# One fused attention and MLP kernel: the first group's load cut in two, and the third output block postponed in the last steps

## The chip, the cores and the metric

The kernel runs on one core of one Trainium2 chip. The metric is the device time of one execution in microseconds (us), here the median of several. Three runs of the kernel before gave 478.76, 478.81 and 479.46 us, so the median is 478.81 us.

## The reference

A linear attention with decay runs over 768 positions for 4 batches and 8 heads of width 48. Its output, 3072 rows of 384 numbers, goes through an MLP: a product to 2048 hidden numbers, an exact GELU, and a product back to 384.

```
for t in range(S):
    cur = np.einsum('bhd,bhe->bhde', u[None] * kt, vt)
    y[:, :, t] = np.einsum('bhd,bhde->bhe', rt, state + cur)
    state = w[None, :, :, None] * state + np.einsum('bhd,bhe->bhde', kt, vt)
h = x @ w_in
g = 0.5 * h * (1.0 + erf(h * inv_sqrt2))
return (g @ w_out).astype(np.float32)
```

All inputs and the output are 32-bit floats.

## The kernel before

The 768 positions are cut into 6 chunks of 128 positions; a chunk with its 4 batches is 512 rows, the free size of a matmul. Attention runs in groups, one for two heads in one chunk, so a chunk has four groups. The MLP runs in 96 steps, 16 for each chunk, one for each block of 128 hidden numbers.

**A step of the MLP.** `moe1` makes 9 matmuls of 128x512 (line 695): three blocks of the input, each as a product of high and low parts (`wh` with the high part, `wl` with the high part, `wh` with the low part). They are summed in the one PSUM bank `Hp`. ScalarE applies the GELU twice, to `gh` (rounded, line 725) and to `gf` (full, line 726), and VectorE forms the remainder `gl` (line 727). `moe2` makes 9 more matmuls (line 737) from `gh` and `gl` into the output banks `O0`, `O1`, `O2`, which hold the three blocks of 128 output columns. `moe2` of a step stands behind `moe1` of the next, so that TensorE has work while the GELU runs. In the last chunk the third block lies half in `O2` (256 rows) and half in the bank `Y` (256 rows).

**The end.** In the last steps of the program the third block is left out of `moe2` and done behind the others. In the kernel before this holds for the last four steps (hidden blocks 12 to 15): the line `range(len(parts) if m < NSTEP - 4 else 2)`, and the list of pairs in the branch `m == NSTEP - 1`, where a pair `(q, i)` is block part `i` (0 and 1 are `O0` and `O1`, 2 is `O2`, 3 is `Y`) of the step `q` before the last. Values that are read so late need buffers that no later step writes: `hidden` gives the last three steps parts of `xx0`. When a bank has its last product, ScalarE (line 775) or VectorE (line 772) copies it out and SP issues its transfer to memory (line 778).

**The front.** Before the first MLP step the four groups of the first chunk are computed. For each group SP loads receptances and keys (`T`, 128 partitions by 4 KB, line 263). VectorE multiplies them to `RK` (line 464), TensorE sums `RK` with `u` in `Hp` (line 469), ScalarE copies the sums to `cs` (line 474) and scales a diagonal with them (`Am`, line 414). VectorE also scales `T` by powers of the decay to `Ts` (line 458), TensorE makes scores from that (line 483), and VectorE puts them into `Am` (line 488). The tables `E` are filled by SBUF transfers from `W` (line 365). The MLP weights come as `raw` (line 379) and are split by ScalarE and VectorE into `wh` and `wl`.

**What sets the order.** All work is recorded with `add` and `dma` into a `Plan`, with an estimated duration, a due time and names for what it reads and writes. `Plan.play` then puts it out by engine, the most urgent of the ready operations first. Its DMA estimates are the constants `DMA_*`; a transfer holds one of eight lanes until it has landed, and the ninth waits for the first one's lane. The queue of SP is in order, and so are all engines.

Of the kernel before, what the change touches and what calls it, by code (L numbers as in the profile page):

```python
# [10 lines left out]
F32R = mybir.dt.float32r  # L11
# [27 lines left out]
LATER = 10 ** 7  # L39
FIRST, STEP, STEP_LAST = 27000, 8400, 3900  # L40
WEIGHT_AHEAD, GROUP_AHEAD, GROUP_DUE = 26000, 28000, 18000
HEATS, HEAT_NS, HEAT_ROOM, MM = 10, 300, 100, 233
WIDE = 96
POOL_DUE, POOL_CLASH = 8000, 550
# [4 lines left out]
AT_LOADS, AT_E = 14000, 15000  # L49

SCALE = ("dd", "d", "d", "d")
PRODUCT = ("d", "d", "d", "d")
BONUS = ("aa", "aa", "aa", "ad")


class Plan:
# [6 lines left out]
    LAG = {"pe": 220, "act": 140, "dve": 115, "pool": 90, "sp": 0, "do": 0}  # L63
    DMA_GAP, DMA_LEAD, DMA_FIXED, DMA_LANES = 480, 1050, 950, 8
    DMA_EARLY, DMA_RATES = 5000, (400.0, 345.0)
    DMA_QUEUED, DMA_SPREAD = 1200, 1050

    def __init__(self, after):
        self.after = after
# [39 lines left out]
    def play(self, due):  # L109
# [11 lines left out]
        for _ in ops:  # L121
            best, clash = None, float("inf")
            for e in self.LAG:
                wait, can = waiting[e], able[e]
                if not wait and not can:
                    continue
                start = max(free[e], lanes[0]) if e == "sp" else free[e]
                while wait and wait[0][0] <= start:
                    n = heapq.heappop(wait)[1]
                    heapq.heappush(can, (due[n], n))  # L130
                if can:
                    n = can[0][1]
                else:
                    start = wait[0][0]
                    n = min((due[n], n) for at, n in wait if at == start)[1]
                if e == "dve":
                    clash = start if ops[n][5] else start + ops[n][1]
                if ops[n][5]:
                    start = max(start, locked["pool" if e == "dve" else "dve"])
                if e == "pool" and best and start + ops[n][1] > clash + POOL_CLASH and due[n] > start + POOL_DUE:  # L140
                    continue
                if best is None or start < best[0]:
                    best = (start, e, n)
            start, e, n = best
            while e == "pe" and heating:
                at = {b: max([free[e]] + [clear.get(x, 0.0) for x in b]) for b in self.heats
                      if not any(unread.get(x, 0) for x in b)}
                b = min(at, key=at.get, default=None)
                if b is None or at[b] + self.heat_room >= start:
                    break  # L150
                self.heats[b]()
                free[e] = at[b] + self.heat_ns
            if able[e]:
                heapq.heappop(able[e])
            else:
                waiting[e].remove((ready[n], n))
                heapq.heapify(waiting[e])
            _, ns, _, fn, _, port = ops[n]
            if e == "sp":
                free[e] = start + self.DMA_GAP  # L160
                queued = bus - start - self.DMA_LEAD
                bus = max(bus, start + self.DMA_LEAD) + ns / self.DMA_RATES[start >= self.DMA_EARLY]
                end = bus + self.DMA_FIXED + self.DMA_SPREAD * (queued > self.DMA_QUEUED)
                lanes = lanes[1:] + [end]
            else:
                free[e] = end = start + ns
            ins = fn()
            if port:
                locked[e] = end
                if e == "dve":  # L170
                    held = ins
                elif held is not None:
                    self.after(ins, held, "port")
            if n in (self.heat_from, self.heat_to):
                heating = n == self.heat_from
            if heating:
                for b in [x for bank in self.heats for x in bank]:
                    if b in self.writes[n]:
                        unread[b] = unread.get(b, 0) + sum(b in self.reads[m] for m in self.users[n])
                    if b in self.reads[n]:  # L180
                        unread[b] = unread.get(b, 0) - 1
                        clear[b] = end + self.LAG[e]
            for m in self.users[n]:
                ready[m] = max(ready[m], end + self.lag(n, m))
                left[m] -= 1
                if not left[m]:
                    heapq.heappush(waiting[ops[m][0]], (ready[m], m))


def rwkv_gelu_mlp(tc, rkT, rkv, wuT, uN, wmlp, r, k, vT, w, u, out):  # L190
    nc = tc.nc
    with ExitStack() as ctx:
# [37 lines left out]
        Am = [sb([C, 2, NB, C], F32, f"Am{i}") for i in range(2)] + [sb([C, 2, NB, C], F32, f"Am{i}", pro) for i in (2, 3)]  # L230
        cs = [sb([C, NB * 2], F32, f"cs{i}") for i in range(4)]
        xx = [sb([128, 2, 3, TOK], F32R, f"xx{i}") for i in range(2)]
        x3 = sb([LP, 2, TOK], F32R, "x3")
        gh = [sb([128, TOK], F32R, f"gh{i}") for i in range(2)]
        gl = [sb([128, TOK], F32R, f"gl{i}") for i in range(2)]
        gf = sb([128, TOK], F32, "gf")
# [21 lines left out]
        slot = lambda gi: gi if gi < NP else NP + gi % 2  # L258


        def load_group(gi, at, r=()):
            s = slot(gi)
            dma(C * 4096, at, lambda: nc.sync.dma_start(T[s], rkT[gi]), r=r, w=[f"T{s}"])
            if gi < NP:
                dma(C * 3072, AT_LOADS + 800 * gi, lambda: nc.sync.dma_start(N[s], rkv[gi, :, 1:]), r=r, w=[f"Nk{s}", f"Nv{s}"])
            else:
                dma(C * 4608, at + 1, lambda: nc.sync.dma_start(N[s], rkv[gi]), r=r, w=[f"Nr{s}", f"Nk{s}", f"Nv{s}"])
# [32 lines left out]
        add("act", 520, LATER, spread_ones, r=["ident", "zeros"], w=["spread"])  # L300


        def heat(dst):
            nc.tensor.matmul(dst, lhsT=zeros[:, 0:128], rhs=zeros, start=True, stop=True)

# [6 lines left out]
                out=x.bitcast(F32).rearrange("p (a n) -> p a n", a=2),  # L312
                in_=zeros[:, 0:DM].bitcast(F32).unsqueeze(1).to_broadcast([128, 2, DM])), r=["zeros"], w=["wa"])

        plan.heats, plan.heat_ns, plan.heat_room = {("H",): lambda: heat(Hp), ("O0",): lambda: heat(O[0])}, HEAT_NS, HEAT_ROOM
        plan.heat_from = add("pe", 430 * HEATS, 10, warm_up, r=["zeros"], w=["H", "A0", "A1", "O0", "O1", "O2", "Y", "U"])


        def powers():
# [124 lines left out]
        def first_group(gi, at, XX, XB, y, YB):  # L444
# [8 lines left out]
            for i, e in enumerate(halves):  # L453
# [4 lines left out]
                    lambda mul=mul, bs=bs, nb=nb: mul(  # L458
                        out=t[:, :, bs], in0=T[gi][:LP, :, bs],
                        in1=W[:, p, 0:C].unsqueeze(1).unsqueeze(1).to_broadcast([LP, 2, nb, C]), op=ALU.mult),  # L460
                    r=["P", f"W{p}", f"T{gi}"], w=[f"{TR}{b}" for b in range(bs.start, bs.stop)], port=True)
            me = PRODUCT[gi]
            mul = nc.vector.tensor_tensor if me == "d" else nc.gpsimd.tensor_tensor
            add("dve" if me == "d" else "pool", dve(512) if me == "d" else pool(512), LATER, lambda: mul(
                out=RK[gi], in0=T[gi][:LP, 0, :, ::-1], in1=T[gi][:LP, 1], op=ALU.mult), r=[f"T{gi}"], w=[f"RK{gi}"], port=True)

            def sum_pairs():
                for b in range(NB):
                    nc.tensor.matmul(
                        Hp[:, WIDE * b:WIDE * b + WIDE].rearrange("s (n j) -> s n j", j=2), lhsT=RK[gi][:, b, :],  # L470
                        rhs=u_pair[:, p, :].unsqueeze(1).to_broadcast([LP, WIDE // 2, 2]), start=True, stop=True)

            add("pe", 1070, LATER, sum_pairs, r=[f"RK{gi}", "w_sb"], w=["H"])
            add("act", 110, LATER, lambda: nc.scalar.copy(
                out=sums.rearrange("s (b j) -> s b j", j=2),
                in_=Hp[:, 0:NB * WIDE].rearrange("s (b x) -> s b x", x=WIDE)[:, :, 0:2]), r=["H"], w=[CS])
            for j in range(2):
                bonus(am, AM, diag, ["diag"], C, sums, CS, j, BONUS[gi][j])
            def scores(bs):
# [13 lines left out]

            def gaps():
                for a in range(2):
                    nc.tensor.matmul(y, lhsT=spread[:, p, :], rhs=x3[:, a, :], start=(a == 0), stop=False,
                                     skip_group_check=True)

            def new():
# [197 lines left out]

        def hidden(m):

            if m < NSTEP - 3:  # L700
                return gh[m % 2], gl[m % 2], f"gh{m % 2}", f"gl{m % 2}"
            i, k_ = NCH % 2, NSTEP - 1 - m
            return xx[i][:, 0, k_], xx[i][:, 1, k_], f"xx{i}{k_}h", f"xx{i}{k_}l"

        def moe1(m, at):
# [8 lines left out]
            if m == 0:  # L714
                gaps0 = lambda k_: gaps[2 * k_:2 * k_ + 2]
                for k_ in range(3):
                    first = add("pe", 3 * MM, at + k_, lambda k_=k_: [
                        product1(x, j, n, (k_,), k_ == 0 and n == 0, k_ == 2 and n == 2) for n in range(3)],
                        r=["wh0", "wl0"] + xr("h", (k_,)) + xr("l", (k_,)) + gaps0(k_), w=["H"])
                    plan.heat_to = plan.heat_to or first  # L720
            else:
                for n in range(3):
# [17 lines left out]
        def moe2(m, at, dest):  # L740
# [14 lines left out]
                        go(m, n, which, at + n)  # L755
            elif m < NSTEP - 2:
                for n in range(3):
                    go(m, n, range(len(parts) if m < NSTEP - 4 else 2), at + n + 2000 * (m == NSTEP - 3 and n == 2))
            elif m == NSTEP - 1:
                for q, i in ((1, 0), (1, 1), (3, 2), (3, 3), (0, 0), (0, 1), (2, 2), (1, 2), (0, 2), (2, 3), (1, 3), (0, 3)):  # L760
                    at += 2000
                    for n in range(3):
                        go(m - q, n, (i,), at + n)
# [110 lines left out]
        def swap():  # L874
# [5 lines left out]
            late.tile([128, 8], F32, name="pad")  # L880

        add("do", 0, SWAP_DUE, swap, w=["late", "ident", "ones", "diag", "past", "P", "WKs", "WN", "zeros", "warm", "spread"] +
            [f"{x}{i}" for x in ("W", "T", "RK", "Nk", "Nv") for i in range(NP)] +
            [f"Ts{i}{b}" for i in range(NP) for b in range(NB)] + [f"Am{i}{j}" for i in (2, 3) for j in range(2)])

        def step_at(m):
            return FIRST + STEP * min(m, 5 * NJ) + STEP_LAST * max(m - 5 * NJ, 0)
# [116 lines left out]
```

## Time and profile before

| | before |
|---|---|
| median of 3 runs | 478.81 us |
| profiled execution, its own time | 479.26 us |
| its span | 477.4 us |
| TensorE busy | 469.3 us (98% of the span) |
| VectorE busy | 229.1 us (48%) |
| ScalarE busy | 182.1 us (38%) |
| GpSimd busy | 67.5 us (14%) |
| mean DMA rate | 98 GB/s |

Busy time says little by itself here: an engine that is full over the whole span (TensorE) sets the length of the middle, and the two ends, where it is not full, have to be read by themselves. The granted TensorE clock was 0.999 over the execution. The chain that ended last is by engine 92% TensorE, 4% DMA and 3% ScalarE.

### The profile page before, as it was taken

Reading aid. Unit: us, or ns where it says so; the run is one execution under the profiler, and the core shown is the slowest. Engines: PE = TensorE matmul, PEld = TensorE weight load, DVE = VectorE, ACT = ScalarE, POOL = GpSimd, SP = SyncE. Lnnn points to the kernel's source line nnn. Section 1 sums busy time; section 2 is a strip of 40 time slices with the busy share of each in tenths; the row PEclk is TensorE's granted clock in tenths of the full one; section 3 lists DMA queues with packets and bytes.
Section 4 is the critical chain, followed back from the end, with each engine's and each line's share of the span. In section 5 each row is a group of like instructions: output and inputs, shape, how many; then the busy total and the mean of one; then the engine's idle time right before and its main releaser. Section 6 shows DMA issues by size and latency. Waiting matters only on the chain.

```text
span 477.4 us, 10280 instructions
## 1 busy us (share of the span) xinstructions
PE 469.3 (98%) x4525; PEld 378.5 (79%) x4525; DVE 229.1 (48%) x345; ACT 182.1 (38%) x333; POOL 67.5 (14%) x91
## 2 busy tenths in 40 slices
PE   8999999999999999999999999999999999999995
PEld 6777788888888787888888888888888887888885
DVE  7989989744354366153543543544335311211111
ACT  9998897233222223222223222223322222322221
POOL 1331021221020222010202202202102000000000
PEclk9999999999999999999999999999999999999999
DMA  8979682414023034031231330311402000100002
GB/s 307 364 288 331 215 266 89 122 51 152 27 80 106 2 116 150 1 106 42 65 106 67 95 104 3 106 65 46 158 19 88 14 0 12 66 1 1 1 0 71
DMA packets 15426, 46.60 MB, mean 98 GB/s; under 512 B 3664, under 2 KB 4048, under 8 KB 15376
## 3 DMA queue, kind: packets, MB, share of 16 engines
q1 hardware_dynamic: 15376, 45.88, 28.6%
q8 instruction: 37, 0.61, 0.5%
q14 instruction: 13, 0.11, 0.1%
HBM read 38.73 MB, written 4.72 MB: 91 GB/s over the span
## 4 chain that ended last, share of the span: by engine, by line
PE 92%; DMA 4%; ACT 3%; issue 0%; DVE 0%; ACTq 0%
PE Hp L695 42%; PE O L737 41%; PE Y L605 2%; DMA E<-W 2%; PE A L613 2%; PE Y L633 2%; PE A L622 1%; DMA raw<-in_wmlp_dram 1%; PE Y L737 1%; ACT W L343 0%; ACT Sa L529 0%; ACT wa L311 0%; ACT L290 0%; ACT wa L394 0%; ACT gh L725 0%; ACT gf L726 0%
## 5 line engine op out<-in xcount | busy, mean ns | idle before, releaser
L695 PE MATMUL Hp<-xx,wh 128*128 128x512 f32 x570 | 167.1, 400 | 0.0
L727 DVE TENSOR_TENSOR gl<-gf,gh 128x512 fp32r<-128x512 f32 x93 | 66.1, 710 | 172.9 <-ACT gf L726 172.7
L725 ACT ACTIVATE gh<-Hp 128x512 fp32r<-128x512 f32 x92 | 54.9, 597 | 217.6 <-PE Hp L695 217.6
L695 PEld LDWEIGHTS Hp<-xx,wh 128*128 128x128 f32 x570 | 104.4, 188 | 25.4 <-ACT gf L726 1.0
L695 PE MATMUL Hp<-xx,wl 128*128 128x512 f32 x285 | 82.0, 395 | 0.0
L737 PE MATMUL O<-gh,wh 128*128 128x512 f32 (+1 forms) x279 | 79.1, 391 | 0.6 <-ACT gf L726 0.6
L737 PE MATMUL O<-gh,wl 128*128 128x512 f32 (+1 forms) x279 | 79.2, 391 | 0.0
L737 PE MATMUL O<-gl,wh 128*128 128x512 f32 (+1 forms) x279 | 78.9, 390 | 0.0
L695 PEld LDWEIGHTS Hp<-xx,wl 128*128 128x128 f32 x285 | 53.6, 188 | 12.7
L737 PEld LDWEIGHTS O<-gh,wh 128*128 128x128 f32 x279 | 52.3, 188 | 13.8 <-ACT gf L726 1.0
L737 PEld LDWEIGHTS O<-gh,wl 128*128 128x128 f32 x279 | 51.6, 188 | 11.7
L737 PEld LDWEIGHTS O<-gl,wh 128*128 128x128 f32 x279 | 51.4, 188 | 11.6 <-issue 0.5
L726 ACT ACTIVATE gf<-Hp 128x512 f32<-128x512 f32 x95 | 56.4, 594 | 0.0
L560 POOL TENSOR_TENSOR Nb<-Nb 128x384 f32<-128x384 f32 x20 | 20.3, 1016 | 123.2 <-DMA Nb<-in_rkv_dram 73.8
L557 DVE TENSOR_TENSOR Tb<-Tb,E 112x1024 f32<-112x1024 f32 x20 | 25.3, 1266 | 2.1 <-DMA Tb<-in_rkT_dram 2.1
L662 DVE SCALAR_TENSOR_TENSOR Sb<-Sa,E,A 48x192 f32<-48x192 f32 x40 | 16.5, 413 | 18.1 <-PE A L622 17.5
L432 ACT CAST xx<-Y 112x512 fp32r<-112x512 f32 x15 | 8.8, 586 | 39.0 <-PE Y L633 39.0
L563 POOL TENSOR_TENSOR Nb<-Nb,WN 128x384 f32<-128x384 f32 x20 | 20.3, 1015 | 21.2 <-DVE wl L406 7.8
L566 POOL TENSOR_TENSOR Nb<-Nb,u_sb 128x384 f32<-128x384 f32 x20 | 20.3, 1013 | 18.3 <-DVE gl L727 13.1
L569 DVE TENSOR_REDUCE cs<-Nb 128x8 f32<-128x384 f32 x20 | 11.1, 553 | 18.1 <-POOL Nb L566 15.8
L643 POOL MEMSET done<- 1x1 f32 x19 | 1.7, 88 | 126.1 <-PE Y L605 126.1
L669 DVE COPY_PREDICATED Am<-past,A 128x512 f32<-128x512 uint32 x20 | 15.0, 748 | 7.0 <-PE A L622 6.8
(114 smaller groups left out, 383.4 us busy)
## 6 DMA issues: line engine op xcount, KB each, us to landing
raw<-in_wmlp_dram SPq DMA_DIRECT2D x16, 767.8 KB, 5.9
Nb<-in_rkv_dram SPq DMA_DIRECT2D x20, 576.0 KB, 5.5
Tb<-in_rkT_dram SPq DMA_DIRECT2D x20, 512.0 KB, 4.3
out_dram<-raw SPq DMA_DIRECT2D x5, 768.0 KB, 3.6
T<-in_rkT_dram SPq DMA_DIRECT2D x4, 512.0 KB, 5.0
xx<-x SPq DMA_DIRECT2D x30, 64.0 KB, 4.0
N<-in_rkv_dram SPq DMA_DIRECT2D x4, 384.0 KB, 7.0
out_dram<-raw SPq DMA_DIRECT2D x2, 256.0 KB, 4.3
```

The source lines that it names most:

```text
L557: add("dve", 1140, LATER, lambda: nc.vector.tensor_tensor(out=flat, in0=flat, in1=E[:, p, 0].rearrange("l h i -> l (h i)").unsqueeze(1).to ...
L560: add("pool", pool(DM), LATER, lambda: nc.gpsimd.tensor_tensor(out=n[:, 0], in0=n[:, 0], in1=n[:, 1], op=ALU.mult), r=[NK], w=[NR])
L563: add("pool", pool(DM), LATER, lambda: nc.gpsimd.tensor_tensor(out=kn, in0=kn, in1=WN2[:, p].rearrange("s j d -> s (j d)").unsqueeze(1).to ...
L566: add("pool", pool(DM), LATER, lambda: nc.gpsimd.tensor_tensor(out=n[:, 0], in0=n[:, 0], in1=u_sb[:, p, :].unsqueeze(1).to_broadcast([C, N ...
L569: add("dve", 465, LATER, lambda: nc.vector.tensor_reduce(out=sums, in_=n[:, 0].rearrange("s b (j d) -> s (b j) d", d=D), axis=AX.X, op=ALU ...
L662: add("dve", 430, at, lambda l=l, x=x: nc.vector.scalar_tensor_tensor(out=out[quarter(1 - x)], in0=src[l], scalar=E[l, p, 1, h, 32:33], in ...
L669: add("dve", 625, LATER, lambda: nc.vector.copy_predicated(out=am, mask=past2.bitcast(U32).unsqueeze(1).unsqueeze(1).to_broadcast([C, 2, N ...
L695: nc.tensor.matmul(dst, lhsT=wt[j][:, 0, k_ * 128:(k_ + 1) * 128], rhs=x[:, a, k_, :], start=start and k_ == ks[0], stop=stop and k_ == ks ...
L725: add("act", 480, LATER, lambda: nc.scalar.activation(out=high, in_=dst, func=AF.Gelu, scale=256.0), r=[H_], w=[GH])
L726: add("act", 480, LATER, lambda: nc.scalar.activation(out=gf, in_=dst, func=AF.Gelu, scale=256.0), r=[H_], w=["gf"])
L727: add("dve", dve(512), LATER, lambda: nc.vector.tensor_tensor(out=low, in0=gf, in1=high.bitcast(F32), op=ALU.subtract), r=["gf", GH], w=[G ...
L737: nc.tensor.matmul(dst[:, a:b], lhsT=wt[j][:, 1, d * 128:(d + 1) * 128], rhs=gt[:, a:b], start=(j == 0 and n == 0), stop=(j == NJ - 1 and ...
```

## The change

There are two parts.

*In the front*, the load of `T` for group 0 becomes two transfers of 256 KB, batches 0 and 1 and then batches 2 and 3. In each partition a half is two runs of 1 KB, where the whole was one run of 4 KB. The product `RK` and the sums of group 0 are recorded by halves as well. The names that the planner uses for `T`, `RK` and `H` are now by batch, and the planner's own DMA estimate gets one more constant.

*At the end*, the third block is left out of `moe2` in the last six steps and not four (`LEFT = 6`), and done behind the others. Hidden block 10 is now kept in `x3`, which grows from 112 to 128 partitions for it; blocks 11 and 12 stay in `gh1` and `gh0`.

```diff
+LEFT = 6
-    DMA_QUEUED, DMA_SPREAD = 1200, 1050
+    DMA_QUEUED, DMA_SPREAD, DMA_UNEVEN = 1200, 1050, 550
...
-                end = bus + self.DMA_FIXED + self.DMA_SPREAD * (queued > self.DMA_QUEUED)
+                end = bus + self.DMA_FIXED + (self.DMA_SPREAD if queued > self.DMA_QUEUED else self.DMA_UNEVEN * (ns > 200000))
...
-        x3 = sb([LP, 2, TOK], F32R, "x3")
+        x3 = sb([128, 2, TOK], F32R, "x3")
...
+        halves_of = lambda gi: ((0, 1), (2, 3)) if gi == 0 else (range(NB),)
...
-            dma(C * 4096, at, lambda: nc.sync.dma_start(T[s], rkT[gi]), r=r, w=[f"T{s}"])
+            for bs in halves_of(gi):
+                dma(C * 1024 * len(bs), at, lambda bs=slice(bs[0], bs[-1] + 1): nc.sync.dma_start(
+                    T[s][:, :, bs], rkT[gi, :, :, bs]), r=r, w=[f"T{s}{b}" for b in bs] if gi < NP else [f"T{s}"])
...
-            add("dve" if me == "d" else "pool", dve(512) if me == "d" else pool(512), LATER, lambda: mul(
-                out=RK[gi], in0=T[gi][:LP, 0, :, ::-1], in1=T[gi][:LP, 1], op=ALU.mult), r=[f"T{gi}"], w=[f"RK{gi}"], port=True)
...
+            for bs in halves_of(gi):
+                sl, Tn, Rn = slice(bs[0], bs[-1] + 1), [f"T{gi}{b}" for b in bs], [f"RK{gi}{b}" for b in bs]
+                add("dve", dve(128 * len(bs)), LATER, lambda sl=sl: nc.vector.tensor_tensor(
+                    out=RK[gi][:, sl], in0=T[gi][:LP, 0, sl, ::-1], in1=T[gi][:LP, 1, sl], op=ALU.mult),
+                    r=Tn, w=Rn, port=True)
+                add("pe", 268 * len(bs), LATER, lambda bs=bs: sum_pairs(bs), r=Rn + ["w_sb"], w=[f"H{b}" for b in bs])
...
-            if m < NSTEP - 3:
+            i, k_ = NCH % 2, NSTEP - 1 - m
+            if k_ == 5:
+                return x3[:, 0], x3[:, 1], "x3h", "x3l"
+            if k_ >= 3:
                 return gh[m % 2], gl[m % 2], f"gh{m % 2}", f"gl{m % 2}"
...
-                    go(m, n, range(len(parts) if m < NSTEP - 4 else 2), at + n + 2000 * (m == NSTEP - 3 and n == 2))
+                    go(m, n, range(len(parts) if m < NSTEP - LEFT else 2), at + n + 2000 * (m == NSTEP - 3 and n == 2))
...
-                for q, i in ((1, 0), (1, 1), (3, 2), (3, 3), (0, 0), (0, 1), (2, 2), (1, 2), (0, 2), (2, 3), (1, 3), (0, 3)):
+                for q, i in ((1, 0), (1, 1), (5, 2), (4, 2), (0, 0), (0, 1), *((q, 2) for q in range(LEFT - 3, -1, -1)),
+                             *((q, 3) for q in range(LEFT - 1, -1, -1))):
```

In the order of instructions the change touches few places. On SP, at the start, the first five transfers were

```order
1 L269 DMA wu_sb_73<-in_wuT_dram 112x12
2 L263 DMA T0_93<-in_rkT_dram 128x1024
3 L263 DMA T1_94<-in_rkT_dram 128x1024
4 L263 DMA T2_95<-in_rkT_dram 128x1024
5 L265 DMA N0_107<-in_rkv_dram 128x768
```

and they are now

```order
1 L273 DMA wu_sb_73<-in_wuT_dram 112x12
2 L266 DMA T0_93<-in_rkT_dram 128x2x256 x2
3 L266 DMA T1_94<-in_rkT_dram 128x1024
4 L266 DMA T2_95<-in_rkT_dram 128x1024
5 L269 DMA N0_107<-in_rkv_dram 128x768
```

One transfer more stands ahead of all the others, whose order is unchanged. On VectorE, at the same place, `RK0` stood between the reciprocals of the decay powers as one instruction

```order
11 L332 RECIPROCAL W_89<-W_89 112x64
12 L464 TENSOR_TENSOR RK0_103<-T0_93 112x512
13 L332 RECIPROCAL W_89<-W_89 112x64 x3
14 L458 TENSOR_TENSOR Ts0_99<-T0_93,W_89 112x2x256 x2
15 L464 TENSOR_TENSOR RK1_104<-T1_94 112x512
```

and now stands there as two. ScalarE and GpSimd keep their order in the front, and TensorE too.

On TensorE, at the end, behind the last products of `O1` for hidden block 14 (`wh14`, `wl14`) there stood

```order
L737 MATMUL O2_72<-gh0_124,wh12_450 128x256
L737 MATMUL O2_72<-gh0_124,wl12_451 128x256
L737 MATMUL O2_72<-gl0_126,wh12_450 128x256
L737 MATMUL Y_68<-gh0_124,wh12_450 128x256
L737 MATMUL Y_68<-gh0_124,wl12_451 128x256
L737 MATMUL Y_68<-gl0_126,wh12_450 128x256
L737 MATMUL O0_70<-xx0_121,wh15_456 128x512
L737 MATMUL O0_70<-xx0_121,wl15_457 128x512
L737 MATMUL O0_70<-xx0_121,wh15_456 128x512
```

and now there stand

```order
L746 MATMUL O2_72<-x3_123,wh10_448 128x256
L746 MATMUL O2_72<-x3_123,wl10_449 128x256
L746 MATMUL O2_72<-x3_123,wh10_448 128x256
L746 MATMUL O2_72<-gh1_125,wh11_450 128x256
L746 MATMUL O2_72<-gh1_125,wl11_451 128x256
L746 MATMUL O2_72<-gl1_127,wh11_450 128x256
L746 MATMUL O0_70<-xx0_121,wh15_458 128x512
L746 MATMUL O0_70<-xx0_121,wl15_459 128x512
L746 MATMUL O0_70<-xx0_121,wh15_458 128x512
```

Six products of 256 rows stand there as before, for other hidden blocks. Behind the last product of `O1` there follow 9 products of `O2` and 9 of `Y` before, and 12 of `O2` and 18 of `Y` now. The 12 products more are those that left the `moe2` of hidden blocks 10 and 11; the number of matmuls is the same.

## Rows read from the trace of the kernel before

**Rows 1.** The page's head.

```profile
span 477.4 us, 10280 instructions
```

**Rows 2.** By stretch: length, busy PE, PEld, DVE, ACT, POOL, PEclk, DMA share, GB/s.

```profile
32.00:36.00 4.00, 4.00 (x78) 3.13 (x77) 3.67 (x8) 3.84 (x6) 2.47 (x3) 1.00 0.26 56
```

**Rows 3.** Chain that ended last, the front: start us, us, what.

```profile
7.75 11.30 DMA E<-W
...
19.06 5.94 DMA raw<-in_wmlp_dram
...
25.02 1.10 ACT wa L394
...
31.02 0.50 ACT gf L726
...
31.56 0.96 PE O L737 x3
```

**Rows 4.** Timeline of the front: start us, us, engine, what [idle before <-releaser].

```profile
5.13 0.69 DVE L464 TENSOR_TENSOR RK<-T 112x512 f32<-112x512 f32 x1 [0.50 <-DMA T<-in_rkT_dram]
...
5.90 1.12 PE L469 MATMUL Hp<-wu_sb,RK 112*128 112x96 f32 x8
...
6.98 0.50 ACT L286 COPY past<-past 64x64 f32<-64x64 f32 x2
...
7.50 0.17 ACT L474 COPY cs<-Hp 128x8 f32<-128x8 f32 x1
...
10.24 1.30 DVE L488 COPY_PREDICATED Am<-past,A 128x1024 f32<-128x1024 uint32 x1 [0.25 <-ACT Am L414]
```

**Rows 5.** DMA queue: packets, MB, share of 16 engines; at 5-5.5, 16-18, 474-474.5 us.

```profile
q1 hardware_dynamic: 54, 0.21, 103.6%
...
q1 hardware_dynamic: 1685, 0.60, 122.4%
...
q1 hardware_dynamic: 138, 0.13, 76.5%
```

**Rows 6.** Chain that ended last, the end.

```profile
457.68 2.09 PE Hp L695 x9
...
461.17 2.14 PE Hp L695 x9
...
471.41 1.07 PE Y L737 x9
```

**Rows 7.** Issues of the first and last output transfer, and their us to landing.

```profile
470.31 0.34 SPq L778 DMA_DIRECT2D out_dram<-raw  x1
out_dram<-raw SPq DMA_DIRECT2D x1, 256.0 KB, 4.4
...
472.99 0.51 SPq L778 DMA_DIRECT2D out_dram<-Nb  x1
out_dram<-Nb SPq DMA_DIRECT2D x1, 128.0 KB, 2.9
```

**Rows 8.** Page, DMA issues (KB each, median us to landing); stretches as in Rows 2.

```profile
out_dram<-raw SPq DMA_DIRECT2D x5, 768.0 KB, 3.6
xx<-x SPq DMA_DIRECT2D x30, 64.0 KB, 4.0
...
108.00:108.50 0.50, 0.50 (x4) 0.41 (x3) 0.00 (x0) 0.50 (x2) 0.00 (x0) 1.00 0.99 381
...
474.00:474.50 0.50, 0.00 (x0) 0.00 (x0) 0.00 (x0) 0.00 (x0) 0.00 (x0) 1.00 0.77 264
```

**Rows 9.** DMA queues at 474.5-475 us, then at 475-475.5 us.

```profile
q1 hardware_dynamic: 13, 0.01, 8.4%
q14 instruction: 1, 0.01, 7.1%
...
q8 instruction: 1, 0.02, 13.1%
q1 hardware_dynamic: 13, 0.01, 6.5%
```

More of the change, by code (lines that the diff above doesn't have):

```diff
@@ L51 @@
 SCALE = ("dd", "d", "d", "d")
-PRODUCT = ("d", "d", "d", "d")
 BONUS = ("aa", "aa", "aa", "ad")
@@ L300, in rwkv_gelu_mlp @@
         add("act", 520, LATER, spread_ones, r=["ident", "zeros"], w=["spread"])
+        HB = [f"H{b}" for b in range(NB)]
         def heat(dst):
@@ L313, in rwkv_gelu_mlp @@
                 in_=zeros[:, 0:DM].bitcast(F32).unsqueeze(1).to_broadcast([128, 2, DM])), r=["zeros"], w=["wa"])
-        plan.heats, plan.heat_ns, plan.heat_room = {("H",): lambda: heat(Hp), ("O0",): lambda: heat(O[0])}, HEAT_NS, HEAT_ROOM
-        plan.heat_from = add("pe", 430 * HEATS, 10, warm_up, r=["zeros"], w=["H", "A0", "A1", "O0", "O1", "O2", "Y", "U"])
+        plan.heats, plan.heat_ns, plan.heat_room = {tuple(HB): lambda: heat(Hp), ("O0",): lambda: heat(O[0])}, HEAT_NS, HEAT_ROOM
+        plan.heat_from = add("pe", 430 * HEATS, 10, warm_up, r=["zeros"], w=["H", *HB, "A0", "A1", "O0", "O1", "O2", "Y", "U"])
         def powers():
@@ L460, in first_group, with sum_pairs @@
                         in1=W[:, p, 0:C].unsqueeze(1).unsqueeze(1).to_broadcast([LP, 2, nb, C]), op=ALU.mult),
-                    r=["P", f"W{p}", f"T{gi}"], w=[f"{TR}{b}" for b in range(bs.start, bs.stop)], port=True)
-            me = PRODUCT[gi]
-            mul = nc.vector.tensor_tensor if me == "d" else nc.gpsimd.tensor_tensor
-            add("dve" if me == "d" else "pool", dve(512) if me == "d" else pool(512), LATER, lambda: mul(
-                out=RK[gi], in0=T[gi][:LP, 0, :, ::-1], in1=T[gi][:LP, 1], op=ALU.mult), r=[f"T{gi}"], w=[f"RK{gi}"], port=True)
-            def sum_pairs():
-                for b in range(NB):
+                    r=["P", f"W{p}"] + [f"T{gi}{b}" for b in range(bs.start, bs.stop)],
+                    w=[f"{TR}{b}" for b in range(bs.start, bs.stop)], port=True)
+            def sum_pairs(bs):
+                for b in bs:
                     nc.tensor.matmul(
@@ L471, in sum_pairs @@
                         rhs=u_pair[:, p, :].unsqueeze(1).to_broadcast([LP, WIDE // 2, 2]), start=True, stop=True)
-            add("pe", 1070, LATER, sum_pairs, r=[f"RK{gi}", "w_sb"], w=["H"])
+            for bs in halves_of(gi):
[4 more added lines that the diff above has]
+                add("pe", 268 * len(bs), LATER, lambda bs=bs: sum_pairs(bs), r=Rn + ["w_sb"], w=[f"H{b}" for b in bs])
             add("act", 110, LATER, lambda: nc.scalar.copy(
                 out=sums.rearrange("s (b j) -> s b j", j=2),
-                in_=Hp[:, 0:NB * WIDE].rearrange("s (b x) -> s b x", x=WIDE)[:, :, 0:2]), r=["H"], w=[CS])
+                in_=Hp[:, 0:NB * WIDE].rearrange("s (b x) -> s b x", x=WIDE)[:, :, 0:2]), r=[f"H{b}" for b in range(NB)], w=[CS])
             for j in range(2):
@@ L495, in gaps @@
                 for a in range(2):
-                    nc.tensor.matmul(y, lhsT=spread[:, p, :], rhs=x3[:, a, :], start=(a == 0), stop=False,
+                    nc.tensor.matmul(y, lhsT=spread[:, p, :], rhs=x3[:LP, a, :], start=(a == 0), stop=False,
                                      skip_group_check=True)
@@ L698, in hidden @@
         def hidden(m):
-            if m < NSTEP - 3:
+            i, k_ = NCH % 2, NSTEP - 1 - m
+            if k_ == 5:
+                return x3[:, 0], x3[:, 1], "x3h", "x3l"
+            if k_ >= 3:
                 return gh[m % 2], gl[m % 2], f"gh{m % 2}", f"gl{m % 2}"
-            i, k_ = NCH % 2, NSTEP - 1 - m
             return xx[i][:, 0, k_], xx[i][:, 1, k_], f"xx{i}{k_}h", f"xx{i}{k_}l"
@@ L718, in moe1 @@
                         product1(x, j, n, (k_,), k_ == 0 and n == 0, k_ == 2 and n == 2) for n in range(3)],
-                        r=["wh0", "wl0"] + xr("h", (k_,)) + xr("l", (k_,)) + gaps0(k_), w=["H"])
+                        r=["wh0", "wl0"] + xr("h", (k_,)) + xr("l", (k_,)) + gaps0(k_), w=["H"] + HB)
                     plan.heat_to = plan.heat_to or first
@@ L882, in rwkv_gelu_mlp @@
         add("do", 0, SWAP_DUE, swap, w=["late", "ident", "ones", "diag", "past", "P", "WKs", "WN", "zeros", "warm", "spread"] +
-            [f"{x}{i}" for x in ("W", "T", "RK", "Nk", "Nv") for i in range(NP)] +
-            [f"Ts{i}{b}" for i in range(NP) for b in range(NB)] + [f"Am{i}{j}" for i in (2, 3) for j in range(2)])
+            [f"{x}{i}" for x in ("W", "Nk", "Nv") for i in range(NP)] +
+            [f"{x}{i}{b}" for x in ("T", "RK", "Ts") for i in range(NP) for b in range(NB)] + [f"Am{i}{j}" for i in (2, 3) for j in range(2)])
         def step_at(m):
```

## The prediction

> **What bounds the kernel now.** I read the page's head and shares first, then the chain of waits from both ends, then the timelines and the DMA queues of the two places that the change touches. The reader is to see three stages.
>
> From about 32 us to 472.5 us TensorE is full: in the first stretch after the front it is busy for 4.00 of 4.00 us [rows 2], and the chain runs from matmul to matmul. There, only matmul work that disappears or a stall that appears counts, and whatever moves the start of this stage moves the end by as much.
>
> In the front, the chain does not run through group 0. It runs through the DMA queue: the tables `E` land at 19.05 us, the third weight block is issued behind them and lands at 25.00 us, ScalarE splits it from 25.02 us and works on without a gap until 31.52 us, and TensorE starts at 31.56 us [rows 3]. The queue is full by then: at 5 us its packets fill 103.6% of the 16 engines [rows 5]. So the third weight block comes when the bytes ahead of it are through.
>
> At the end, TensorE finishes at 472.48 us [rows 6], the last bank is copied out and its transfer issued at 472.99 us. It lands 2.9 us later, at 475.9 us, and the first output transfer, issued at 470.31 us, lands only at 474.7 us [rows 7]. The span ends at 477.4 us [rows 1], 1.5 us behind the last landing; I take these 1.5 us, and the 1.86 us between the span and the execution's own 479.26 us, as unchanged.
>
> **The front, part by part.** The product `RK0` waits 0.50 us for its load and starts at 5.13 us [rows 4], so VectorE could have begun at 4.63 us. Two halves at half of 0.69 us each: the first can run as soon as half of the bytes are there, the second still waits for 5.1 us or a little more. VectorE is through some 0.1 to 0.3 us earlier. This I cost at nothing, because of two covers. The sums end at 5.90 + 1.12 = 7.02 us, but ScalarE copies masks until 7.48 us and takes the sums only at 7.50 us [rows 4]; its order is unchanged. And VectorE's next joint with ScalarE is at 10.24 us, where it already waits 0.25 us for `Am` [rows 4]: what it gains before only lengthens this wait. If both covers were gone, 0.3 us would be the most that could come through, and the wait for the third weight block at 25.02 us would hold even that back: the bytes ahead of it are the same. So no gain.
>
> The price is in packets. The load was 128 packets of 4 KB and becomes 512 of 1 KB. At 5 us, 0.21 MB took 103.6% of 16 engines for 0.5 us, 8.3 engine-us, or 39.5 ns per thousand bytes and 162 ns for a 4 KB packet. At 474 us nearly all of 138 packets are of 1 KB, and they took 76.5% of 8 engine-us, 44 ns each [rows 5]. So 512 x 44 = 22.5 engine-us stand against 128 x 162 = 20.7; the 1.8 more over 16 engines are **+0.11 us**, paid by everything behind in the full queue, the third weight block among it, and so by TensorE's start. The bounds: 0 if the engines overlap packets; and, by the dearest packets that the trace has, the 1638 of 256 B that are most of the queue's 1685 at 16 to 18 us (39.2 engine-us, less 7 for the other 0.18 MB, leaves 20 ns each, 77 ns per thousand bytes [rows 5]), (77 - 39.5) x 524 / 16 = 1.2 us. I take the 1 KB row, since these packets have that size. SP issues one transfer more, 0.4 to 0.5 us; the queue ahead of the third weight block is deep enough to hide that (it needs 5.94 us from issue to landing [rows 3]).
>
> On this place the Trainium skill speaks against the change. Its page Perfetto Trace Analysis, section DMA Optimizations, says that splitting may help where the DMA engines are generally idle, and that transfers under 2 KB have much overhead each. The row at 5 us shows them full; the page has no price, and by it the front could only lose.
>
> **The end, part by part.** Hidden blocks 10 and 11 lose six products of 256 rows each in their `moe2`, and 12 of them appear behind `O1`. A product of 256 rows is 1.07 / 9 = 0.119 us [rows 6], so 1.43 us leave the steps and come back: 0. But `moe1` of the next step must wait until the GELU has read `Hp`, and only the shorter `moe2` stands between. The trace has this twice already: the nine matmuls take 2.14 us there and 2.09 us in a full step [rows 6]. Two more such steps: **+0.09 us**. `x3`, `gh` and `gl` are written by no later step, so nothing waits for them.
>
> What is gained is time between the early output transfers and the last. `O0` and `O1` are complete 12 x 0.119 = 1.4 us earlier, measured from the end of TensorE, and `O2` 9 x 0.119 = 1.1 us earlier. The last transfer, of 128 KB from `Y`, is issued at the same distance from the end. Does it land sooner? Nearly all its bytes move between 474.0 and 474.5 us (264 GB/s, 0.13 MB [rows 5, 8]), yet it lands at 475.9 us. In the microsecond after 474.5 us the queue has 26 packets left, 13 in each half, at 8.4% and 6.5% of 16 engines, which is about one engine [rows 9]. So one engine is late with its share of all four transfers, and in this time instruction packets run beside it, one of 7.1% (0.57 us of an engine) and one of 13.1% (1.05 us). With `O0`, `O1` and `O2` out of its way an engine has only its eight packets of `Y` left, 8 x 44 ns = 0.35 us, and the last landing would follow the bulk.
>
> The bounds: alone and undisturbed, a transfer of 768 KB lands in 3.6 us and moves at 381 GB/s [rows 8], which is 2.06 us for its 786 thousand bytes and 1.5 us besides. 128 KB would need 1.5 + 0.35 = 1.9 us and land 1.0 us earlier than 2.9 us. The other end is no gain: a transfer of 64 KB inside SBUF takes 4.0 us with the queue nearly empty [rows 8]. I take **-0.75 us**, nearer to the row of the same direction, less half of an instruction packet of 0.57 us in the way.
>
> Of this the Trainium skill gives another size. DMA: Bandwidth & Descriptors, section "Anatomy of one DMA", fits 2.0 us and the bytes over 436 GB/s for transfers issued by GpSimd, most of it the wait for the write's receipt; as an estimate from that page 128 KB take 2.3 us, the gain is 0.6 us and the sum by it would be -0.4 us.
>
> **Sum.** +0.11 + 0.09 - 0.75 = -0.55 us. The profiled execution, 479.26 us, would become 478.7; it lies 0.45 us above the median, and the median becomes 478.81 - 0.55 = **478.3 us**.
>
> **Rivals.**
> - *The end pays in full and the front costs nothing.* For it: packets in the front add to more than 100%, so engines overlap them. Against: instruction packets are seen in the last two microseconds. -1.0 + 0.09 = -0.9: 477.9 us.
> - *The last transfer's time is its own.* Its place is the landing of `Y`: if 2.9 us is what a write of 128 KB needs at this point, whether through its receipt or through instruction packets that come with the end of the engines' programs, nothing is gained and the two costs stay: +0.11 + 0.09 = +0.2, 479.0 us, slower than before. It decides once the end gives back less than 0.2 us. For it: the 64 KB transfers at 4.0 us. Against: the 768 KB row.
> - *The receipt takes most of it*, the size that the page named above leads to. From rows, halfway between no gain and 1.0 us: -0.5 + 0.2 = -0.3, 478.5 us.
> - *The 1 KB packets are as dear as the 256 B ones.* +1.2 + 0.09 - 0.75 = +0.5, 479.3 us. For it: no row has 1 KB packets on their way into SBUF. Against: the 44 ns row.
>
> That `RK0` does not start earlier at all would change no number here.
>
> **Chances and range.** Forecast 0.47, full pay 0.17, own time 0.17, receipt 0.13, dear packets 0.06. A measurement tells some 0.2% from no change, 0.96 us. Below 477.85 us lie 0.6 of the full pay and a sixth of the forecast's spread: 0.18 faster. Above 479.77 us lie half of the dear packets and a sixth of the own-time case: 0.06 slower. The rest, 0.76, is within. The range reaches from the full pay with 0.4 us to spare, 477.5 us, to the dear packets, 479.3 us.
>
> **What would show it.** In the profile after: the first half of `RK0` starts between 4.6 and 5.0 us, ScalarE's copy of the sums still at 7.5 us; the chain still runs through `E`, the third weight block and ScalarE, and TensorE is released at 31.6 to 31.8 us. Four shortened steps have `moe1` at 2.14 us. The output transfer of `O0` is issued 4.1 us ahead of the last, which lands in 1.9 to 2.4 us. I am wrong if the third weight block lands earlier or TensorE starts before 31.4 us; if the last transfer still needs 2.9 us; or if TensorE waits at some new place in the last six steps.

## The result and the profile after

The changed kernel takes 482.50 us (median of 20 runs, 479.92 to 483.52) against 479.24 us of the kernel before on the same chip: ratio 1.0057, 95% interval 1.0049 to 1.0066. It is slower, by some 3 us. One of these 20 executions of before took 655.49 us, and one of the merge further down 1384.55 us; single ones like these do not move a median. The profiled execution of the changed kernel took 480.5 us with a span of 478.7 us, 1.3 us above the span of before [rows 1] and near the lower end of its own runs; a second trace further down shows one of 483.26 us.

The chain of waits, front, in the kernel after (start us, us, what), runs through the same places as [rows 3]:

```profile
9.50 10.62 DMA E<-W
...
20.14 6.48 DMA raw<-in_wmlp_dram
...
26.64 1.10 ACT wa L400
...
32.65 0.50 ACT gf L735
...
33.19 0.97 PE O L746 x3
```

Everything is the chain of before, moved: `E` is issued 1.75 us later, TensorE is released at 33.19 instead of 31.56 us. The timeline of the same place, answering to [rows 4]:

```profile
4.60 0.41 DVE L477 TENSOR_TENSOR RK<-T 112x256 f32<-112x256 f32 x1
...
5.72 0.43 DVE L477 TENSOR_TENSOR RK<-T 112x256 f32<-112x256 f32 x1 [0.71 <-DMA T<-in_rkT_dram]
5.86 1.03 PE L471 MATMUL Hp<-wu_sb,RK 112*128 112x96 f32 x8
...
7.50 0.17 ACT L481 COPY cs<-Hp 128x8 f32<-128x8 f32 x1
```

The first half starts early, the second later than the whole product did, and ScalarE takes the sums at 7.50 us as before. So in this execution the product by halves moved nothing behind it. SyncE's queue shows where the time went. Issues of before, and then of after:

```profile
1.28 0.41 SPq L263 DMA_DIRECT2D T<-in_rkT_dram  x1
1.74 0.43 SPq L263 DMA_DIRECT2D T<-in_rkT_dram  x1
...
7.75 0.78 SPq L365 DMA_DIRECT2D E<-W  x1
```

```profile
1.28 0.71 SPq L266 DMA_DIRECT2D T<-in_rkT_dram  x1
2.03 0.60 SPq L266 DMA_DIRECT2D T<-in_rkT_dram  x1
2.67 0.60 SPq L266 DMA_DIRECT2D T<-in_rkT_dram  x1
3.31 0.43 SPq L266 DMA_DIRECT2D T<-in_rkT_dram  x1
...
4.73 0.83 SPq L266 DMA_DIRECT2D T<-in_rkT_dram  x1
...
9.50 0.74 SPq L371 DMA_DIRECT2D E<-W  x1
```

The two halves take 0.71 and 0.60 us to issue instead of 0.41, the next load 0.60 as well, and the fourth group's 0.83 against 0.46. And `E` is not issued when SyncE is free, but when an earlier load has landed: of the eight lanes it takes over the one of the third group's load (fourth and twelfth transfer before, fifth and thirteenth after). This load is issued at 2.21 us before and at 3.31 us after; its way to landing (KB, us), before and then after:

```profile
T<-in_rkT_dram SPq DMA_DIRECT2D x1, 512.0 KB, 5.4
T<-in_rkT_dram SPq DMA_DIRECT2D x1, 512.0 KB, 6.1
```

So it lands at some 7.6 and 9.4 us: 1.1 us of the delay is the later issue, 0.7 us the longer way. SyncE's wait for `E` (total, times, longest us), first 16 us, before and then after; before, the profile puts it down to VectorE's `Ts`, whose end comes as late as the landing:

```profile
SPq L365 <- DVE Ts L458: 1.0, 1, 1.0
SPq L371 <- DMA T<-in_rkT_dram: 1.0, 1, 1.0
```

The queue itself (packets, MB, share of 16 engines) moves less from 2 to 8 us, first before, then after, there with its stretches 4.5 to 5 and 5 to 5.5 us, where [rows 5] had 0.21 MB:

```profile
q1 hardware_dynamic: 628, 2.04, 94.9%
```

```profile
q1 hardware_dynamic: 864, 1.50, 83.0%
...
q1 hardware_dynamic: 81, 0.09, 112.1%
...
q1 hardware_dynamic: 28, 0.07, 80.0%
```

0.54 MB less by 8 us; at the 0.42 MB per us that before reaches at 5 us [rows 5], this is 1.3 us of the 1.63 us. Most of it is not lost while the queue fills: from 2 to 4 us it moves 0.39 MB before and 0.32 MB after. From 4 to 8 us, before and then after:

```profile
q1 hardware_dynamic: 501, 1.65, 101.6%
q1 hardware_dynamic: 481, 1.18, 98.7%
```

There the packets fill the time of the engines in both kernels, but those of after need more of it for their bytes. The end of the chain, answering to [rows 6]:

```profile
454.47 2.13 PE Hp L702 x9
...
461.55 2.15 PE Hp L702 x9
...
467.24 4.85 PE O L746 x30
472.09 2.05 PE Y L746 x18
```

The first and the last output transfer, answering to [rows 7]:

```profile
470.68 0.34 SPq L788 DMA_DIRECT2D out_dram<-raw  x1
out_dram<-raw SPq DMA_DIRECT2D x1, 256.0 KB, 2.0
...
474.65 0.33 SPq L788 DMA_DIRECT2D out_dram<-Nb  x1
out_dram<-Nb SPq DMA_DIRECT2D x1, 128.0 KB, 2.6
```

From release to TensorE's end it is 440.95 us, before 440.92. From there to the end of the span 4.56 us, before 4.92. So the spans differ by +1.63 + 0.03 - 0.36 = +1.3 us.

### The profile page after: what moved, and what is told of

Read it like the earlier page. It is cut to its first block, busy times and chain, and to the rows that moved or that the text cites. A ratio compares the mean times of both kernels' runs of the same rounds, so it can differ in the third digit from the quotient of the medians.

```text
span 478.7 us, 10286 instructions
## 1 busy us (share of the span) xinstructions
PE 469.6 (98%) x4525; PEld 378.4 (79%) x4525; DVE 228.2 (48%) x346; ACT 182.2 (38%) x333; POOL 67.6 (14%) x91
## 4 chain that ended last, share of the span: by engine, by line
PE 92%; DMA 4%; ACT 3%; issue 0%; DVE 0%; ACTq 0%
PE Hp L702 42%; PE O L746 41%; PE Y L612 2%; DMA E<-W 2%; PE A L620 2%; PE Y L640 2%; PE A L629 1%; DMA raw<-in_wmlp_dram 1%; PE Y L746 1%; ACT W L349 0%; ACT Am L420 0%; ACT Sa L536 0%; ACT wa L317 0%; ACT L294 0%; ACT wa L400 0%; ACT gh L734 0%
```

## The experiments

Each stands beside runs of the kernel before on the same chip, whose medians lie between 479.20 and 479.29 us, and at 479.96 us for the 64 empty bytes. A time is a median; behind it stands the ratio to before with its 95% interval, which is not the quotient of the two medians. "By 8 us" is what the queue moved from 2 to 8 us. Besides the lines shown, the order of instructions is that of before, or of the change where its end is in.

**The two parts apart.** Front of the change with the end of before, and the reverse (`halves_of` without halves):

```diff
-LEFT = 6
+LEFT = 4
...
-        halves_of = lambda gi: ((0, 1), (2, 3)) if gi == 0 else (range(NB),)
+        halves_of = lambda gi: (range(NB),)
```

> The front of the change alone (the first group's load in two transfers, product and sums by halves), the end as before. Theory A: 2.5 to 4 us above the kernel before, with the third weight block landing 1.5 us late or more and TensorE's release as late. Rival B (the end carries the loss): within 0.5 us of the kernel before.

> The end of the change alone (third block left out of the last six steps), the front as before. Theory A (the whole loss is in the front): TensorE is released at 31.6 us as before, TensorE ends 0.0 to 0.1 us later, the last output transfer lands in 2.2 to 2.6 us and not 2.9 us; the time is 0.2 to 0.5 us under the kernel before. Rival B (the end costs time): the time is 0.5 us or more above the kernel before.

Front alone: 482.36, ratio 1.0058 (1.0038 to 1.0078), 1.60 MB by 8 us. End alone: 479.06, ratio 0.9994 (0.9976 to 1.0012); in its trace the last transfer lands after 2.3 us, and TensorE's end stands 4.27 us ahead of the span's. The whole loss is the front's. But 2.3 us is no gain by the end: in the traces of the 13 other runs that keep the end of before, front alone among them, the last transfer lands after 2.4 to 2.6 us, and the 2.9 us of the first trace is the exception. In the run with the halves of the product only, for one:

```profile
out_dram<-Nb SPq DMA_DIRECT2D x1, 128.0 KB, 2.5
```

**Packets or transfers.** The first group in one transfer of 512 packets of 1 KB (the tile laid out in memory for it), and in two of 64 partitions each with packets of 4 KB, product whole:

```diff
+            if gi == 0:
+                load = lambda: [nc.sync.dma_start(T[0][l:l + 64], rkT[0, l:l + 64]) for l in (0, 64)]
```

> The kernel before with one thing changed: the first group's keys and receptances lie in memory as four blocks, so the one transfer of 512 KB consists of 512 packets of 1 KB and not 128 of 4 KB; the product and everything else as before. Theory A1 (short packets into a cold queue are the price, by their number): 2 to 4 us above the kernel before, and SP needs 0.6 us or more to issue this transfer. Theory A2 (the additional transfer is the price): within 0.5 us of the kernel before. My priced packets (the prediction's row): 0.1 us.

> The kernel before with one thing changed: the first group's load as two transfers of 64 partitions each, with packets of 4 KB as before; the product whole, behind both. Theory A1 (short packets): within 0.5 us of the kernel before, the queue moves at over 300 GB/s from 3.5 us on. Theory A2 (one transfer more, with its issue and its lane): 2 to 4 us above the kernel before.

One transfer with small packets: 479.67, ratio 0.9998 (0.9980 to 1.0015). Two with large ones: 480.43, ratio 1.0033 (1.0008 to 1.0059), 1.58 MB by 8 us. In one transfer the packets are not the price. Two transfers cost 1.2 us here, not the 2 to 4 us that I expected.

**The form of the issue.** The compiled program marks transfers as prepared: the whole loads of before have the mark, the one load of 1 KB packets too; the change's halves (two runs of 1 KB per partition) and the 64-partition ones lack it. Two prepared halves (2 KB each, by layout; product and sums by halves; then also with the change's end), and the whole load of before without the mark:

```diff
+                    nc.dge_precook = False
+                    i = nc.sync.dma_start(T[0], rkT[0])
+                    nc.dge_precook = True
```

> The front of the change alone, with the first group laid out in memory so that each half is one run of 2 KB in every partition: still two transfers, product and sums by halves, instruction order as in the front alone. The compiled program then marks both halves as prepared ahead for the queue, like before's whole tiles, which the change's halves are not. Theory A (the form of the issue is the price: 0.59 to 0.71 us instead of 0.41 to 0.43 for each unprepared one and the next, and the queue starved in its first 6 us): issues of 0.41 to 0.45, embedding rows issued 0.4 to 0.5 us later than before (8.2 to 8.5), TensorE released at 31.6 to 32.5, time within 0.5 us of before (478.7 to 479.7). Theory B (any split of the first load, or one more transfer in the empty queue, is dear): 1.5 to 3 us slower than before (480.7 to 482.3), release at 33 or later. Theory C (the product and the sums by halves disturb the front): also 481 or more, although the loads land as before.

> The whole change with the halves laid out as runs of 2 KB, so that both loads are prepared; the end as in the change. Theory A: the front costs nothing, or 0.4 us, against before, and the end gives its 0.4 to 0.65 us: 478.4 to 479.2, faster than the change by 3 us or more and level with before or up to 0.6 us faster. Theory B: as slow as the change, 481 to 482.5.

> Before, with the first group's load whole, of 4 KB packets, in one transfer, but kept off the prepared form; nothing else differs. Theory A (form of the issue): its issue takes 0.6 to 0.7 us instead of 0.41, the next one 0.55 to 0.6, data start 0.3 to 0.5 us later, embedding rows issued 0.4 to 0.5 us later, release 0.5 to 1 us later, time 0.4 to 1.2 us over before (479.6 to 480.4), about half of what two unprepared halves cost. Theory B (the number of transfers or the packets): no difference, within 0.2 us of before (479.0 to 479.4).

One unprepared issue: 0.61 us, the next 0.58, the load lands 4.2 us behind its issue and not 3.8, time 479.66, ratio 1.0010 (0.9999 to 1.0022), about what the theory said, and not sure to be more than nothing. But the prepared halves still cost: 480.79, ratio 1.0037 (1.0022 to 1.0052), with the end 480.69, 1.0030 (1.0019 to 1.0042). My theory A, by which they cost at most 0.5 us, held for half of the loss at most. The prepared halves are issued quickly, but a later issue stretches (SyncE's issues, first half and fourth group's load):

```profile
1.29 0.41 SPq L269 DMA_DIRECT2D T<-in_rkT_dram  x1
...
4.38 1.49 SPq L269 DMA_DIRECT2D T<-in_rkT_dram  x1
```

**Split, halves, place.** Only the load split (keys, then receptances, 2 KB each, prepared), on the first or on the second group; only product and sums by halves; the change's unprepared split on the fourth group:

```diff
+            if gi == 0:   # second run: 1
+                load = lambda: [nc.sync.dma_start(T[s][:, a], rkT[gi, :, a]) for a in (0, 1)]
...
+            if gi == 3:
+                load = lambda: [nc.sync.dma_start(T[s][:, :, b:b + 2], rkT[gi, :, :, b:b + 2]) for b in (0, 2)]
```

> Before, with the first group's load in two transfers of 2 KB packets, keys first and receptances behind them; both carry the mark of the prepared form, and product, sums and the order of all else are those of before. Theory D (two transfers where there was one, while the queue is still empty, cost by themselves): 2 MB moved by 8 us fall to 1.7, issues of the seventh to tenth transfer stretch to 0.6 to 1.5 us, release of TensorE 1 to 2 us later, time 480.2 to 481.3, as with the prepared halves. Theory C (the product and the sums by halves on VectorE and TensorE cost it): nothing lost, 478.9 to 479.6.

> The same split of keys and receptances, prepared, on the second group's load, the third transfer of the queue, instead of the first's. Theory D1 (any transfer more among the first few, whichever load is split): as the split of the first load, 480.2 to 481.3. Theory D2 (only the very first load counts, because it is the one whose data the empty queue waits for): within 0.4 us of before, 478.9 to 479.6, as when the seventh transfer was split.

> Before, with the first group's load in one transfer and only the product and the sums by halves. Theory D: nothing happens to the queue, 2.0 MB moved by 8 us, time 478.9 to 479.6. Theory C: 480.2 to 481.3, bytes moved by 8 us 1.7 MB.

> Before, with the fourth group's load (the seventh transfer of the queue, issued at 3.8) in the change's two halves of 1 KB packets instead of the first group's; product and sums whole. Theory A, in its second part (an unprepared issue is dear only while the queue is empty): both issues take 0.6 to 0.8 us, embedding rows are issued 0.7 to 1 us later, but 2 MB are queued ahead by then, so the bytes moved by 8 us stay at 2.0 MB and the time within 0.5 us of before (478.9 to 479.7). Rival B (each unprepared issue costs its own length wherever it stands, by the issue of the embedding rows): release 0.8 to 1.2 us later, time 480.0 to 480.5. Rival C (1 KB packets themselves slow the queue): bytes moved by 8 us fall by 0.2 MB or more, time 479.7 to 480.5.

First group: 480.65, ratio 1.0034 (1.0022 to 1.0046). Second: 480.23, 1.0025 (1.0013 to 1.0037). Halves without a split: 479.25, 1.0011 (0.9994 to 1.0027). Fourth group, with issues of 0.71 and 0.60 us: 479.11, 0.9999 (0.9990 to 1.0008), 2.01 MB by 8 us. So it is the split of an early load. Halving the product costs nothing that shows, and the same unprepared split costs nothing three loads later. In the first-group run the chain leads through other transfers of the same late queue, the first group's values and a piece of `E`:

```profile
3.16 6.94 DMA N<-in_rkv_dram
...
14.27 6.79 DMA E<-W
...
34.08 0.96 PE O L746 x3
```

**The change again.** The same kernel, for a second trace.

> The changed kernel once more, on the chip of these three, for a second trace: its profiled execution was 2 us below its median. If the loss is all in the front, one that takes 482 to 483 us has TensorE's release 1 to 2 us later still (34 to 35.5), and the stretch from release to TensorE's end unchanged at 440.7 to 441.0.

482.08, ratio 1.0050 (1.0030 to 1.0070); profiled at 483.26 us. The second half lands at 7.09 us, and now group 0 itself is on the chain, where it was not in the first trace (chain; the queue from 2 to 8 us stands at 1.28 MB):

```profile
2.03 5.06 DMA T<-in_rkT_dram
...
35.42 0.50 ACT gf L735
```

ScalarE's `gf`, for which TensorE waits, is 2.8 us later than in the first trace, more than the 1 to 2 us that I expected; the time is 2.8 us longer too. TensorE starts at 35.96 us, and its end is 441.05 us behind that, 0.13 us more than in before. By these two traces, what lies between the first profiled execution and the median is more of the same loss.

**Count or size.** One tiny transfer more behind the first load; second and third group merged in one transfer of 1 MB; this merge with the first load split, so that the count is that of before; and the merge with the change's end:

```diff
+                load = lambda: [nc.sync.dma_start(tiny, wuT), nc.sync.dma_start(T[s], rkT[gi])]
...
+        T12 = sb([128, 2, 2, NB, C], F32, "T12", pro)
+                dma(C * 8192, at, lambda: nc.sync.dma_start(T12.rearrange("p g a b c -> p (g a b c)"), src), r=r,
```

> Before, with one transfer more between the first and the second group's loads: the small table of 112 x 12 numbers once again, into a place that nothing reads; prepared form. Theory D (the count of transfers among the first few): 480.0 to 481, TensorE's release 1 us or more later, as with the split loads. Theory F (a transfer costs by being small for its issue of 0.43 us, since the queue gets half the bytes per issue): the issue of 0.47 us with almost no bytes delays all behind it by 0.5 us at most, 479.2 to 479.9. Theory G (the split itself, two transfers into one tile): as before, 479.0 to 479.4.

> Before, with the second and the third group's loads merged into one transfer of 1 MB in runs of 8 KB per partition (the two tiles lie side by side, the data are laid out for it in memory): one transfer fewer. Theory D read backwards: the queue fills faster, 2.1 MB or more by 8 us, release 0.3 to 1 us earlier, time 478.2 to 478.9. Rival: in before the queue already runs at 400 GB/s from 4.5 us on, so nothing is left to gain: 479.0 to 479.5. Against both: products of the second group wait for 1 MB instead of 0.5, 479.6 or more.

> The merge of the second and third group's loads, and the first group's load split in keys and receptances: as many transfers as in before, the first two of 256 KB. Theory D (count): within 0.4 us of before, 478.9 to 479.6. Theory F (a small first transfer feeds the empty queue too slowly, whatever follows): 480.2 to 481, as with the split alone.

> The merge together with the end of the change alone (third column block left behind in the last six steps): if the merge gives 0.3 to 1 us and the end its 0.2 to 0.6, 478.0 to 478.7, faster than before by more than the measurement is uncertain; if the merge gives nothing, 478.8 to 479.2.

Merge: 479.28, ratio 1.0002 (0.9990 to 1.0014), with the end 479.02, 0.9999 (0.9989 to 1.0009): one transfer fewer gives nothing. Merge with the split: 481.92, 1.0047 (1.0028 to 1.0067), so the count as such is not it either; theory D fell, and 481.92 lies above theory F's 480.2 to 481 too. The tiny one was a surprise: 474.74, ratio 0.9908 (0.9885 to 0.9931), although its front is the late one (1.60 MB by 8 us, release at 35.01 us). Its table of 48 bytes had also moved the working tiles in SBUF by 64 bytes.

**64 empty bytes.** The tiles moved, no transfer more; then with the change's end:

```diff
+        sb([128, 16], F32, "pad0")
         w_sb = wu_sb[:, 0:NP]
```

> Before, with 64 bytes per partition left empty ahead of the working tiles, so that hidden states, activations, landing buffers and states stand 64 bytes further on (the places of weights and of the first four groups unchanged); no transfer more, the order of all instructions as in before. Theory P (the place of the moving data sets the pace of the matmuls): 8.1 us less from TensorE's release to its end, release as in before (31.5 to 32.1), time 470.8 to 471.6. Theory Q (something else in the run with the tiny transfer, as TensorE's later start, made it faster): within 0.4 us of before, 478.9 to 479.6. If P, the tiny transfer costs 474.74 less this time, some 3.5 us; if the release here is at 35 as well, the moved landing buffers cost it, and not the transfer.

> The 64 empty bytes together with the end of the change alone. Theory P: 470.2 to 471.4, at or up to 0.6 us under the empty bytes alone, and some 8 us faster than before; theory Q: 478.5 to 479.2.

472.68 (5 runs), ratio 0.9863 (0.9839 to 0.9887), and with the end 473.11 (4 runs), 0.9856 (0.9839 to 0.9874). Both beat both kernels by more than 6 us, and both miss theory P's times by 1 us and more; theory Q is out. Release is at 32.49 us and TensorE's end 433.1 us behind it, 7.8 us less than before. TensorE's groups from 200 to 300 us (busy us, mean ns), before and with the empty bytes:

```profile
L737 PE MATMUL O<-gl,wh 128*128 128x512 f32 x65 | 18.6, 394 | 0.0
L695 PE MATMUL Hp<-xx,wl 128*128 128x512 f32 x63 | 18.0, 395 | 0.0
```

```profile
L745 PE MATMUL O<-gl,wh 128*128 128x512 f32 x63 | 17.7, 389 | 0.0
L703 PE MATMUL Hp<-xx,wl 128*128 128x512 f32 x65 | 18.4, 390 | 0.0
```

5 ns for each of the 1,671 wide matmuls (570, 285, three times 266 and 18 of the last steps, without the halves of 256 rows) is 8.4 us, the size of the gain. Against this kernel the tiny transfer costs 474.74 - 472.68 = 2.1 us, or 2.7 us by the two differences from before. With 5 and 6 runs on two chips this is uncertain by more than 1 us: early in the queue, 5 KB cost about as much as a split.

## Why the prediction was wrong

The step that failed is this one: "SP issues one transfer more, 0.4 to 0.5 us; the queue ahead of the third weight block is deep enough to hide that", with its ground, that the bytes ahead of the block are the same. They are the same, but the block is issued only when `E` has landed, and `E` only when the third group's load has. This load is issued 1.1 us later and needs 0.7 us more, in a queue that moves 1.18 MB from 4 to 8 us where it moved 1.65 MB. I took the full engines at 5 us [rows 5] for a rate that a transfer at 1.3 us could not change. Measured in place of 0: +1.63 us in the profiled execution, some +3 us by the medians.

A second term was mis-sized, the end: -0.75 us rested on the 2.9 us of one trace.

Point by point:
- *Packets, +0.11 us.* Not contradicted: 1 KB packets in one transfer are within 0.2% of before. The rival of dear packets had the right sign, and no run shows its mechanism. By the Trainium skill's rule (Perfetto Trace Analysis, DMA Optimizations) the front could only lose, and it did; but splits with packets of 2 KB and of 4 KB lost too.
- *Covers of the product.* Right as far as they were named: first half at 4.60 us, sums taken at 7.50 us; by halves alone nothing is lost. They fail once the second half lands at 7.09 us.
- *Shortened steps, +0.09 us.* Right for the steps: 2.13 to 2.15 us, and +0.03 us from release to TensorE's end.
- *The end, -0.75 us.* Not shown. Against the first trace of before, the two traces give -0.36 and -0.65 us. But the last transfer lands after 2.3 to 2.6 us in the six traces with the new end, and after 2.4 to 2.6 us in 13 of the 14 with the old one. The timed pairs with and without the new end differ by -0.3 to +0.4 us. So the rival by which this time is the transfer's own fits best. One late DMA engine, as I read the rows, may have made the 2.9 us of that one execution.

The loss has two parts, by the medians: 1.0 to 1.6 us for the split of an early load in itself (prepared halves, keys and receptances, 64 partitions), and about as much again in the change. What the second part is, no run shows. The mark of the prepared form is not enough for it: one unprepared issue measured +0.4 us, and two unprepared transfers of 64 partitions with 4 KB packets cost 1.2 us in all. Two prepared halves with 1 KB packets were not tried.

What stays open is why an early split slows the queue. It is not the count (merge with split), and not the bytes handed over: with prepared halves 1.5 MB are issued by 3.1 us, and the engines still move 0.16 MB per half microsecond at 5 us. Nor is it a queue that fills too slowly. With the second group's load split it moves 0.54 MB from 2 to 4 us, more than the 0.39 MB of before, and loses from 4 to 8 us like the others (2 to 4 us, then 4 to 8 us):

```profile
q1 hardware_dynamic: 178, 0.54, 80.4%
q1 hardware_dynamic: 475, 1.19, 95.1%
```

No view has a row for a single DMA engine, and which of them was late could not be seen.

## What to carry to other kernels

Price a transfer by where it stands in its queue: a split among the first loads cost 1 to 3 us here, the same one three loads later was free. Read a time that a term rests on in more than one execution. Ask of each load which later transfer waits for its landing. And where one kind of matmul fills the span, try its operands at other places in SBUF before trimming microseconds elsewhere.

## What the runs showed of the hardware

- Among the first four transfers of the queue an issue took 0.40 to 0.43 us for 5 KB, 256 KB, 512 KB and 1 MB alike; it took 0.58 to 0.71 us where the program had not marked it as prepared, with 0.58 to 0.60 us for the next one; one marked issue took 0.50 us, behind the load of 1 KB packets. Later in the queue, marked ones stretched too, to 1.49 us.
- With an early split, or 5 KB more, the queue moved 0.97 to 1.31 MB from 4 to 8 us; with whole first loads it was 1.57 to 1.67 MB.
- Tiles of moving data 64 bytes further on (in the program's memory map from a multiple of 128 to one of 128 plus 64, where the weights already were) brought 128x512 matmuls from 394 and 395 to 389 and 390 ns, 1.4% of the kernel. Which of the moved tiles does it was not tried.
- The release of TensorE came between 31.25 and 32.92 us in single executions whose first loads are whole and prepared, so a front is compared by medians and not by one trace.
